# Attention and two MLPs on one core: the low-part subtraction moved from GpSimd to VectorE, some softmax quotients to ScalarE

## The chip, the cores and the metric

The kernel runs on one core of a Trainium2 chip. The metric is the device time of one execution in microseconds. The core has five engines with an instruction queue each: TensorE (PE in the profile; its weight loads are PEld), VectorE (DVE), ScalarE (ACT), GpSimd (POOL) and SyncE (SP), which here only starts DMA transfers.

## The reference

```python
# q, k, v: (4, 8, 576, 64); all inputs and outputs fp32
scores = scale * q @ k.T                      # per batch and head
masks: heads 0-3: 0 <= i - j < 32; heads 4-7: 0 <= i - j < 128 and (i - j) % 4 == 0
attn = softmax(where(mask, scores, -1e9))
x = (attn @ v) reshaped to (2304, 512)
x = relu(x @ w_in) ** 2 @ w_out               # first MLP, 512 -> 2048 -> 512
h = x @ w_in2; out = (h * cos(h)) @ w_out2    # second MLP, same sizes
```

## The kernel before

**Matmuls in parts.** Every fp32 factor of the two MLPs is held as a high part, which TensorE's fast fp32 format holds exactly, and a low part, the rest. A product is three matmuls: high by high, high by low, low by high.

**Weights.** A weight chunk (128 x 512) arrives as 64-bit words over SyncE (`load_w`, line L105; three buffers `raw`). `split_w` makes fp32 words of them with three VectorE instructions (L116, L119, L122) in a tile `wt` with two buffers, ScalarE casts that to the high part (L125), and GpSimd subtracts the high part from `wt` to give the low part (L127). There are 32 chunks for each MLP (16 values of `fc`, `i` = 0 and 1), and the second MLP's chunks go into the tiles of the first's, so each waits until the last block of the first MLP has used the tile.

**Blocks.** The 2304 tokens go through each MLP in five blocks of 512 or 384 (`SIZES`). For each `fc` a block has `product1` (12 matmuls, L306), `middle` and `product2` (12 matmuls, L363). `middle` of the first MLP is a relu (L318), a square (ScalarE L321 or VectorE L337), the high part (ScalarE L346) and the low part (VectorE L348). In the second MLP it has L324, a rounding step on GpSimd (L325), L328, L330, L333, L334, L337, L346 and L348.

**Attention.** It is cut into 48 units. A unit has scores (L198), for the later units a mask (L215), a maximum (L219), three exponentials with row sums on ScalarE (L225), the sum's reciprocal (L230, L231), the quotient (L232), a transpose (L237), a copy (L240), the product with the values (L249) and the two parts of the result (L276 on ScalarE, L278 on VectorE). The first 12 units (`first`) run ahead of the MLP and have their quotient on GpSimd. The other 36 are spread over the blocks of the first MLP, and have theirs on VectorE.

**Order.** Each step is written down at a time `t` counted in steps of `fc` (block k of the first MLP begins at 16 k), and the list is sorted by these times. The stretches before t = 0 and from t = 96 on are issued as written. Between them, where the first MLP and the second one's first block lie, a planner orders each engine's instructions by its own costs, with the written order as priority. `SPLIT` holds the times of the four steps of `split_w` after its start; early chunks (six) have times of their own. Splits are half a step of `fc` apart in the first MLP.

Of the kernel before, what the change touches and what calls it, by code (L numbers as in the profile page):

```python
# [11 lines left out]
AF = mybir.ActivationFunctionType  # L12
ALU = mybir.AluOpType
# [3 lines left out]
P = 128  # L17
# [6 lines left out]
KT = 96  # L24
TPU = 3
# [11 lines left out]
NF = DFF // P  # L37
# [19 lines left out]
def attention_moe_moe(ctx: ExitStack, tc: tile.TileContext, units, masks, ident16_in, ident_in, w1, w2, out):  # L57
    nc = tc.nc
# [16 lines left out]
    f32 = lambda ap: ap.bitcast(F32)  # L75
# [4 lines left out]
    def at(t, f, *a):  # L80
        events.append((t, len(events), f, a))
# [26 lines left out]
    def split_w(m, fc, i):  # L108


        words = raws.pop((m, fc, i))
        low, high = words[:, :, 0], words[:, :, 1]
        parts = wpool.tile([P, 2, DM], F32R, tag=f"w{fc}_{i}", name=f"w{fc}_{i}")
        hi, lo = weights[m, fc, i] = parts[:, 0, :], parts[:, 1, :]
        t = wtmp.tile([P, DM], U32, tag="t", name="wt")
        nc.vector.tensor_scalar(  # L116
            out=t, in0=high, scalar1=3, scalar2=0x3FFFFFF8,
            op0=ALU.logical_shift_left, op1=ALU.bitwise_and)
        nc.vector.scalar_tensor_tensor(  # L119
            out=t, in0=high, scalar=0xC0000000, in1=t, op0=ALU.bitwise_and, op1=ALU.bitwise_or)  # L120
        yield
        nc.vector.scalar_tensor_tensor(  # L122
            out=t, in0=low, scalar=29, in1=t, op0=ALU.logical_shift_right, op1=ALU.bitwise_or)
        yield
        nc.scalar.copy(out=hi, in_=f32(t))  # L125
        yield
        nc.gpsimd.tensor_tensor(out=lo, in0=f32(t), in1=f32(hi), op=ALU.subtract)  # L127
        yield


# [2 lines left out]
    def block(m, k):  # L133
        if (m, k) not in xs:
            s = SLOT[k]
            xs[m, k] = tuple(
                ring.tile([P, NC, SIZES[k]], F32R, tag=f"x{n}{s}", name=f"x{n}{s}") for n in "hl"
            )
        return xs[m, k]
# [32 lines left out]
    def bank():  # L172
        return ps_h.tile([P, 512], F32, tag="h", name="h")

    def y_bank(e):
        return ps_y.tile([P, 512], F32, tag=f"y{e}", name=f"y{e}")

    def warm_up(n):

        spare = bank()  # L180
        for _ in range(n):
            nc.tensor.matmul(spare, idle[:, :P], idle, start=True, stop=True)

    def unit(u):


        first = u < N_EARLY
        b, hp, g = u // UNITS, u % UNITS // NG, u % NG
        dilated = hp >= NPAIR // 2
        x, v = loaded.pop(u)  # L190
        s = bank()[:, :TPU * KT]
        m0 = MASK_OF[dilated][g] * KT
        m = mask[:, m0:m0 + TPU * KT]
        if u == 0:
            warm_up(7)
        for i in range(TPU):
            for j in range(0, P, D):
                nc.tensor.matmul(  # L198
                    s[j:j + D, i * KT:(i + 1) * KT],
                    x[j:j + D, i:UQ:TPU],  # L200
                    x[j:j + D, UQ + i * QT:UQ + i * QT + KT],
                    start=not first or i == 0, stop=not first,
                )
        if first:
            nc.tensor.matmul(s, ident16, m, start=False, stop=True)
        if u == 1:
            warm_up(6)
        yield
        p = ppool.tile([P, TPU, KT], F32, tag="p", name="p")
        scale = 1.0 / D ** 0.5  # L210
        tiles = lambda t: t.rearrange("p (i k) -> p i k", k=KT)
        if first:
            s = tiles(s)
        else:
            nc.vector.scalar_tensor_tensor(  # L215
                out=p, in0=tiles(s), scalar=scale, in1=tiles(m), op0=ALU.mult, op1=ALU.add)
            s, scale = p, 1.0
        nm = stat.tile([P, TPU], F32, tag="nm", name="nm")
        nc.vector.tensor_reduce(out=nm, in_=s, axis=AX.X, op=ALU.max, negate=True)  # L219
        if first:  # L220
            nc.vector.tensor_scalar(out=nm, in0=nm, scalar1=scale, scalar2=None, op0=ALU.mult)
        yield
        sm = stat.tile([P, TPU], F32, tag="sm", name="sm")
        for i in range(TPU):
            nc.scalar.activation(  # L225
                out=p[:, i, :], in_=s[:, i, :], func=AF.Exp, scale=scale,
                bias=nm[:, i:i + 1], accum_out=sm[:, i:i + 1])
        yield
        rs = stat.tile([P, TPU], F32, tag="rs", name="rs")
        nc.vector.tensor_scalar(out=rs, in0=sm, scalar1=EPS, scalar2=None, op0=ALU.add)  # L230
        nc.vector.reciprocal(out=rs, in_=rs)  # L231
        (nc.gpsimd if first else nc.vector).tensor_tensor(  # L232
            out=p, in0=p, in1=rs.unsqueeze(2).to_broadcast([P, TPU, KT]), op=ALU.mult)
        yield
        pt = bank()[:KT, :UP]
        for i in range(TPU):
            nc.tensor.transpose(pt[:, i * 2 * QT:(i + 1) * 2 * QT], p[:, i, :], ident)  # L237
        yield
        pts = ptpool.tile([KT, UP], F32, tag="pts", name="pts")
        nc.scalar.copy(out=pts, in_=pt)  # L240
        yield
        pv = y_bank(u % 4) if first else bank()
        if not first:
            v = loaded.pop(u)
        for i in range(TPU):
            for j in range(2):
                at_q = (i * 2 + j) * QT
                at_v = (i * 2 + j) * D
                nc.tensor.matmul(  # L249
                    pv[j * D:(j + 1) * D, i * QT:(i + 1) * QT],  # L250
                    v[:, at_v:at_v + D],
                    pts[:, at_q:at_q + QT],
                    start=True, stop=True,
                )
        yield

        p0 = g * TPU * QT
        done = 0
        pieces = []
        while done < TPU * QT:  # L260
            if dilated:
                r, i0 = divmod(p0 + done, S // DIL)
                n, step = min(TPU * QT - done, S // DIL - i0), DIL
                t0 = b * S + DIL * i0 + r
            else:
                n, step = TPU * QT - done, 1
                t0 = b * S + p0 + done
            k = max(i for i in range(NB) if STARTS[i] <= t0)
            t0 -= STARTS[k]
            n = min(n, -(-(SIZES[k] - t0) // step))  # L270
            xh, xl = (t[:, hp, t0:t0 + (n - 1) * step + 1:step] for t in block(0, k))
            piece = pv[:, done:done + n]
            pieces.append((xh, xl, piece))
            done += n
        for xh, _, piece in pieces:
            nc.scalar.copy(out=xh, in_=piece)  # L276
        for xh, xl, piece in pieces:
            nc.vector.tensor_tensor(out=xl, in0=piece, in1=f32(xh), op=ALU.subtract)  # L278
        yield
# [10 lines left out]
    def in_steps(times, key, steps, *a):  # L290
        for i, t in enumerate(times):
            at(t, *((resume, key) if i else (start, key, steps, *a)))
# [119 lines left out]
    def needed(u):  # L412
        b, hp, g = u // UNITS, u % UNITS // NG, u % NG
        t = b * S + (g * TPU * QT if hp < NPAIR // 2 else 0)
        return max(i for i in range(NB) if STARTS[i] <= t)

    later = sorted(range(N_EARLY, UNITS * B), key=lambda u: (needed(u), u))
    place = []
    for k, (n, t, span) in enumerate(((10, 0.051, 14.1), (12, -0.15, 13), (10, 0.04, 14), (4, 0.051, 12))):
        place += [k * NF + t + span * i / n for i in range(n)]  # L420

    def later_by(t, d):

        while d:
            k = int(t // NF) if d > 0 else -int(-t // NF) - 1
            pace = PACE[k % NB]
            edge = (k + 1) * NF - t if d > 0 else k * NF - t
            move = d / pace
            if abs(move) <= abs(edge):
                return t + move  # L430
            t += edge
            d -= edge * pace
        return t
    for u in range(UNITS * B):
        if u < N_EARLY:
            t = 1.3 * u if u < 2 else 3.877 + 1.656 * (u - 2)
            times = [before(t + d) for d in (0, 1, 2.07, 2.87, 4.24, 4.95, 5.32, 6.2)]
        else:
            t = place[later.index(u)]
# [6 lines left out]

    EARLY_LOADS = (2.5, 3.5, 6.62, 8.91, 10.16, 11.56)
    EARLY_SPLITS = (5.5, 7, 17.91, 21.32, 23.16, 24.98)
    SPLIT = (0, 0.05, 0.2, 0.3)
    split_at = []  # L450
    for h in range(2 * NF):
        w = (0, h // 2, h % 2)
# [3 lines left out]
        else:  # L456
            t = h / 2 - 1.573
            times = [t + d for d in SPLIT]
            at(split_at[h - 3] + 0.01 if h >= RAW_EARLY + 3 else before(-1. + 0.01 * h), load_w, *w)
# [9 lines left out]
    for h, (t, w) in enumerate(split_at):  # L469
        in_steps([t + d for d in SPLIT], ("w", *w), split_w, *w)  # L470
        at(t - 1.5, load_w, *w)
    for m in range(2):
        for k in range(NB):
            t = (m * NB + k) * NF
# [98 lines left out]
```

## Time and profile before

| | us |
|---|---|
| median of 3 runs | 942.76 (942.71 to 943.51) |
| profiled execution: its time | 943.5 |
| its span, first to last instruction | 941.7 |
| busy PE / DVE / ACT / POOL | 904.4 / 546.8 / 445.5 / 148.9 |
| mean granted TensorE clock | 0.982 of full |

The span is what the trace covers; 1.8 us of the execution's time lie around it. Busy time is the time in which an engine ran at least one instruction. Work that TensorE does at a granted clock below 1 takes longer and counts as busy too.

### The profile page before, as it was taken

What the parts mean: (1) busy time and instruction counts of PE and PEld (TensorE: products, weight loads), DVE (VectorE), ACT (ScalarE), POOL (GpSimd) and SP (SyncE); (2) the same over time, 40 slices, a digit from 0 to 9 for tenths busy, and PEclk for the clock granted to TensorE, in tenths of its full rate; (3) what the DMA queues carried; (4) which work ended last, traced back from release to release, by engine and by line L of the source; (5) the groups of instructions that cost most, each with busy time, mean ns of one, the idle gap of its engine ahead of it and who ended that gap; (6) DMA issues with size and microseconds to landing.
All of it is one profiled execution on the core that took longest, in us unless ns stands there. A gap on an engine that the chain in (4) does not pass through costs nothing.

```text
span 941.7 us, 13625 instructions
## 1 busy us (share of the span) xinstructions
PE 904.4 (96%) x5161; PEld 772.7 (82%) x5161; DVE 546.8 (58%) x1019; ACT 445.5 (47%) x1062; POOL 148.9 (16%) x160
## 2 busy tenths in 40 slices
PE   7898799999999999999987899999999999999998
PEld 5576577999887777888987788889998888888998
DVE  5899962445343435332599887455555565455554
ACT  4765554445343433322444465445554544545553
POOL 2444430000000000000254422111111111111110
PEclk8999899999999999999999899999999999999999
DMA  9756521222121113000456431002002002000100
GB/s 249 219 163 203 181 82 32 94 54 57 29 74 34 44 29 128 1 0 1 145 173 200 130 123 34 1 1 90 1 6 75 1 0 79 1 1 1 45 1 34
DMA packets 27680, 66.28 MB, mean 70 GB/s; under 512 B 3168, under 2 KB 15328, under 8 KB 27616
## 3 DMA queue, kind: packets, MB, share of 16 engines
q1 hardware_dynamic: 27616, 65.42, 22.7%
q8 instruction: 41, 0.67, 0.3%
q14 instruction: 23, 0.19, 0.1%
HBM read 55.97 MB, written 9.44 MB: 69 GB/s over the span
## 4 chain that ended last, share of the span: by engine, by line
PE 68%; DVE 15%; issue 11%; DMA 3%; POOL 1%; ACT 1%; SPq 0%; POOLq 0%; ACTq 0%; DVEq 0%
PE y L363 32%; PE h L306 31%; DVE wt L119 4%; DVE wt L116 3%; DMA early<-units 3%; DVE wt L122 3%; PE h L198 2%; PE h L249 2%; DVE gl L348 1%; PE h L237 1%; POOL kf L325 1%; DVE r L330 1%; POOL w L127 1%; DVE p L232 1%; DVE r L328 1%
## 5 line engine op out<-in xcount | busy, mean ns | idle before, releaser
L363 PE MATMUL y<-gh,w 128*128 128x512 f32 (+1 forms) x1280 | 400.6, 374 | 4.1 <-ACT gh L346 2.1
L306 PE MATMUL h<-xh,w 128*128 128x512 f32 (+1 forms) x1280 | 402.4, 375 | 1.2 <-DVE xl L278 0.9
L363 PEld LDWEIGHTS y<-gh,w 128*128 128x128 f32 x1280 | 240.7, 190 | 36.4 <-ACT gh L346 2.6
L306 PEld LDWEIGHTS h<-xh,w 128*128 128x128 f32 x1280 | 241.1, 190 | 33.8 <-PE y L363 1.3
L363 PE MATMUL y<-gl,w 128*128 128x512 f32 (+1 forms) x640 | 238.5, 373 | 11.3 <-DVE gl L348 11.2
L306 PE MATMUL h<-xl,w 128*128 128x512 f32 (+1 forms) x640 | 238.0, 372 | 0.0
L348 DVE TENSOR_TENSOR gl<-r,gh 128x512 fp32r<-128x512 f32 (+1 forms) x160 | 107.8, 674 | 118.9 <-ACT gh L346 118.5
L337 DVE TENSOR_TENSOR r<-h,r 128x512 f32<-128x512 f32 (+1 forms) x128 | 81.9, 640 | 158.7 <-ACT r L334 96.0
L127 POOL TENSOR_TENSOR w<-wt,w 128x512 fp32r<-128x512 f32 x64 | 93.4, 1463 | 428.2 <-ACT w L125 428.2
L363 PEld LDWEIGHTS y<-gl,w 128*128 128x128 f32 x640 | 121.8, 190 | 28.7 <-DVE gl L348 13.9
L306 PEld LDWEIGHTS h<-xl,w 128*128 128x128 f32 x640 | 121.9, 191 | 14.8
L346 ACT CAST gh<-r 128x512 fp32r<-128x512 f32 (+1 forms) x160 | 92.0, 575 | 88.8 <-PE y L363 72.8
L333 ACT ACTIVATE r<-r 128x512 f32<-128x512 f32 (+1 forms) x80 | 47.2, 590 | 148.1 <-DVE r L330 148.1
L325 POOL TENSOR_SCALAR kf<-kf 128x512 f32<-128x512 f32 (+1 forms) x80 | 47.5, 594 | 327.9 <-ACT kf L324 320.7
L318 ACT ACTIVATE r<-h 128x512 f32<-128x512 f32 (+1 forms) x80 | 44.3, 553 | 96.9 <-PE h L306 96.6
L125 ACT CAST w<-wt 128x512 fp32r<-128x512 f32 x64 | 39.6, 620 | 76.3 <-DVE wt L122 76.1
L122 DVE SCALAR_TENSOR_TENSOR wt<-wraw,wt 128x512 uint32<-128x512 uint32 x58 | 60.9, 1050 | 1.0
L324 ACT ACTIVATE kf<-h,magic 128x512 f32<-128x512 f32 (+1 forms) x80 | 51.1, 639 | 20.9 <-PE h L306 20.0
L334 ACT ACTIVATE r<-r,halfpi 128x512 f32<-128x512 f32 (+1 forms) x80 | 54.5, 681 | 2.5
L225 ACT ACTIVATE p<-p,nm 128x96 f32<-128x96 f32 x108 | 39.5, 366 | 33.2 <-DVE nm L219 33.2
L330 DVE SCALAR_TENSOR_TENSOR r<-kf,r 128x512 f32<-128x512 f32 (+1 forms) x80 | 53.2, 665 | 2.6
L328 DVE SCALAR_TENSOR_TENSOR r<-kf,h 128x512 f32<-128x512 f32 (+1 forms) x80 | 50.1, 626 | 7.8 <-POOL kf L325 7.8
(49 smaller groups left out, 528.2 us busy)
## 6 DMA issues: line engine op xcount, KB each, us to landing
wraw<-w SPq DMA_DIRECT2D x58, 512.0 KB, 3.6
uq<-units SPq DMA_DIRECT2D x36, 208.0 KB, 2.6
uv<-units SPq DMA_DIRECT2D x36, 144.0 KB, 2.2
early<-w SPq DMA_DIRECT2D x6, 512.0 KB, 9.6
y<-o SPq DMA_DIRECT2D x6, 512.0 KB, 2.8
xraw<-y SPq DMA_DIRECT2D x6, 512.0 KB, 4.9
out<-o SPq DMA_DIRECT2D x6, 512.0 KB, 2.8
early<-units SPq DMA_DIRECT2D x12, 208.0 KB, 9.2
```

Source lines behind the costliest of these rows:

```text
L122: nc.vector.scalar_tensor_tensor(out=t, in0=low, scalar=29, in1=t, op0=ALU.logical_shift_right, op1=ALU.bitwise_or)
L127: nc.gpsimd.tensor_tensor(out=lo, in0=f32(t), in1=f32(hi), op=ALU.subtract)
L306: nc.tensor.matmul(h, w[:, c * P:(c + 1) * P], x[:, c, :], start=c == 0 and i == 0, stop=c == NC - 1 and i == 2)
L324: nc.scalar.activation(out=kf, in_=h, func=AF.Identity, bias=magic, scale=INV2PI)
L325: nc.gpsimd.tensor_scalar(out=kf, in0=kf, scalar1=-MAGIC, scalar2=1.0, op0=ALU.add, op1=ALU.mult)
L328: nc.vector.scalar_tensor_tensor(out=r, in0=kf, scalar=-C1, in1=h, op0=ALU.mult, op1=ALU.add)
L330: nc.vector.scalar_tensor_tensor(out=r, in0=kf, scalar=-C2, in1=r, op0=ALU.mult, op1=ALU.add)
L334: nc.scalar.activation(out=r, in_=r, func=AF.Sin, bias=halfpi, scale=-1.0)
L337: nc.vector.tensor_tensor(out=r, in0=h, in1=r, op=ALU.mult)
L346: nc.scalar.copy(out=gh, in_=r)
L348: nc.vector.tensor_tensor(out=gl, in0=r, in1=f32(gh), op=ALU.subtract)
L363: nc.tensor.matmul(y[e], w[:, e * P:(e + 1) * P], g, start=fc == 0 and n == 0, stop=fc == NF - 1 and n == 2,)
```

## The change

The low parts of all weight chunks are subtracted on VectorE, so that it runs all of `split_w` but the cast. The quotient of the first 12 units moves from GpSimd to VectorE. The quotient of the 11 later units that begin beside the first block (`place` below 16) moves from VectorE to ScalarE, as three activations with a scale for each row. The last step of a split is written at 0.62 in place of 0.3. GpSimd has then no work in the first MLP; in the second it keeps L325.

```diff
@@ split_w
         nc.scalar.copy(out=hi, in_=f32(t))
         yield
-        nc.gpsimd.tensor_tensor(out=lo, in0=f32(t), in1=f32(hi), op=ALU.subtract)
+        nc.vector.tensor_tensor(out=lo, in0=f32(t), in1=f32(hi), op=ALU.subtract)
         yield
@@ unit
         nc.vector.reciprocal(out=rs, in_=rs)
-        (nc.gpsimd if first else nc.vector).tensor_tensor(
-            out=p, in0=p, in1=rs.unsqueeze(2).to_broadcast([P, TPU, KT]), op=ALU.mult)
+        if u in with_weights:
+            for i in range(TPU):
+                nc.scalar.activation(
+                    out=p[:, i, :], in_=p[:, i, :], func=AF.Copy, scale=rs[:, i:i + 1])
+        else:
+            nc.vector.tensor_tensor(
+                out=p, in0=p, in1=rs.unsqueeze(2).to_broadcast([P, TPU, KT]), op=ALU.mult)
@@ after place
+    with_weights = {u for u, t in zip(later, place) if t < NF}
@@
-    SPLIT = (0, 0.05, 0.2, 0.3)
+    SPLIT = (0, 0.05, 0.2, 0.62)
```

## Rows read from the trace of the kernel before

**Rows 1.** Stages: length, then each engine's busy time (instructions), clock, DMA share, GB/s.
```profile
10.00:40.00 30.00, 25.52 (x300) 18.80 (x301) 24.19 (x78) 21.52 (x101) 12.02 (x16) 0.89 1.01 280
40.00:130.00 90.00, 76.28 (x463) 58.56 (x461) 87.06 (x152) 49.38 (x139) 41.33 (x29) 0.92 0.52 164
130.00:464.00 334.00, 333.76 (x2097) 279.28 (x2098) 136.61 (x333) 128.07 (x393) 3.83 (x3) 1.00 0.16 48
464.00:538.00 74.00, 62.67 (x322) 59.59 (x321) 70.90 (x86) 33.57 (x66) 34.89 (x24) 0.93 0.55 173
```

**Rows 2.** Chain that ended last, by line: 40 to 130 us, then 464 to 538 us.
```profile
by line: DVE wt L119 20.4%; issue 20.3%; DVE wt L122 17.1%; DVE wt L116 15.7%; DVE p L232 5.6%; DVE gl L348 3.8%; POOL w L127 3.7%; DVE xl L278 3.5%; DVE p L215 3.4%; ACT w L125 2.1%; DVE nm L219 2.0%; DVE rs L230 1.0%; DVE rs L231 0.7%; AC
...
by line: issue 35.5%; DVE wt L119 24.8%; DVE wt L116 15.3%; DVE gl L348 9.5%; DVE wt L122 9.4%; POOL w L127 1.8%; ACT w L125 1.7%; DVE xl L396 1.3%; ACT xh L395 0.7%; PE y L363 0.6%
```

**Rows 3.** Timeline, 68 to 77 us: start, length, engine, instruction.
```profile
68.06 0.68 DVE L122 SCALAR_TENSOR_TENSOR wt<-wraw,wt 128x512 uint32<-128x512 uint32 x1
68.66 0.42 DVE L116 TENSOR_SCALAR wt<-wraw 128x512 uint32<-128x512 uint32 x1
...
69.47 1.49 POOL L127 TENSOR_TENSOR w<-wt,w 128x512 fp32r<-128x512 f32 x1 [3.27 <-ACT w L125]
...
69.84 1.67 DVE L122 SCALAR_TENSOR_TENSOR wt<-wraw,wt 128x512 uint32<-128x512 uint32 x1
...
73.61 0.19 ACT L225 ACTIVATION_READ_ACCUMULATOR p<-p,nm 128x1 f32 x1
...
76.21 0.17 DVE L231 RECIPROCAL rs<-rs 128x3 f32<-128x3 f32 x1
```

**Rows 4.** VectorE's groups, 40 to 130 us: busy us, mean ns, idle before.
```profile
L122 DVE SCALAR_TENSOR_TENSOR wt<-wraw,wt 128x512 uint32<-128x512 uint32 x26 | 26.1, 1004 | 0.2
L119 DVE SCALAR_TENSOR_TENSOR wt<-wraw,wt 128x512 uint32<-128x512 uint32 x26 | 21.2, 820 | 0.3
L116 DVE TENSOR_SCALAR wt<-wraw 128x512 uint32<-128x512 uint32 x26 | 15.4, 599 | 2.4 <-POOL w L127 2.4
L232 DVE TENSOR_TENSOR p<-p,rs 128x288 f32<-128x288 f32 x8 | 10.1, 1261 | 0.0
```

**Rows 5.** VectorE's groups, 200 to 400 us, where GpSimd ran nothing.
```profile
L348 DVE TENSOR_TENSOR gl<-r,gh 128x512 fp32r<-128x512 f32 x23 | 15.9, 690 | 23.3 <-ACT gh L346 23.0
...
L232 DVE TENSOR_TENSOR p<-p,rs 128x288 f32<-128x288 f32 x19 | 8.7, 458 | 0.7
...
L348 DVE TENSOR_TENSOR gl<-r,gh 128x384 fp32r<-128x384 f32 x10 | 5.6, 557 | 11.1 <-ACT gh L346 11.1
...
L122 DVE SCALAR_TENSOR_TENSOR wt<-wraw,wt 128x512 uint32<-128x512 uint32 x2 | 1.4, 688 | 0.0
L116 DVE TENSOR_SCALAR wt<-wraw 128x512 uint32<-128x512 uint32 x2 | 0.8, 418 | 0.0
```

**Rows 6.** VectorE's groups, 464 to 538 us.
```profile
L122 DVE SCALAR_TENSOR_TENSOR wt<-wraw,wt 128x512 uint32<-128x512 uint32 x23 | 27.5, 1195 | 0.7
L119 DVE SCALAR_TENSOR_TENSOR wt<-wraw,wt 128x512 uint32<-128x512 uint32 x23 | 20.1, 872 | 0.7
L116 DVE TENSOR_SCALAR wt<-wraw 128x512 uint32<-128x512 uint32 x23 | 11.8, 511 | 1.3 <-POOL w L127 1.3
L348 DVE TENSOR_TENSOR gl<-r,gh 128x384 fp32r<-128x384 f32 x13 | 11.5, 882 | 1.8 <-ACT gh L346 1.8
```

**Rows 7.** GpSimd's groups: 40 to 130 us, then 464 to 538 us.
```profile
L127 POOL TENSOR_TENSOR w<-wt,w 128x512 fp32r<-128x512 f32 x29 | 43.1, 1490 | 49.9 <-ACT w L125 49.9
...
L127 POOL TENSOR_TENSOR w<-wt,w 128x512 fp32r<-128x512 f32 x24 | 34.9, 1457 | 43.0 <-ACT w L125 43.0
```

**Rows 8.** ScalarE's groups, 40 to 130 us.
```profile
L125 ACT CAST w<-wt 128x512 fp32r<-128x512 f32 x28 | 17.4, 620 | 33.9 <-DVE wt L122 33.8
L225 ACT ACTIVATE p<-p,nm 128x96 f32<-128x96 f32 x24 | 8.8, 366 | 2.4 <-DVE nm L219 2.4
```

**Rows 9.** DMA issues of the whole span: count, size, median us to landing.
```profile
wraw<-w SPq DMA_DIRECT2D x58, 512.0 KB, 3.6
```

## Prediction

> **What bounds the kernel now.** I read first the stages of the span. From 130 to 464 us TensorE is busy 333.76 of 334 us, so nothing done elsewhere in that stretch can shorten it. Two stretches are different: from 40 to 130 us TensorE is idle 13.7 us and VectorE is busy 87.06 of 90, and from 464 to 538 us TensorE is idle 11.3 us and VectorE is busy 70.90 of 74 [rows 1]. These are the stretches in which the weights of the two MLPs are split. TensorE's granted clock is 0.92 and 0.93 of full there, so it spent part of them on the lower of its two levels, behind its own waits [rows 1].
>
> Then the chain that ended last in both. Nearly all of it is VectorE: the three passes of the split and, as "issue", time in which VectorE ran without a release that the profile shows [rows 2]. TensorE stands for less than one per cent of the second. So in these two stretches, 164 us long, the time is VectorE's sum.
>
> Then the length of the same VectorE instruction. L122 takes 0.68 us at 68.06, and 1.67 us at 69.84, where a subtraction of GpSimd that began at 69.47 and ended at 70.96 overlaps it [rows 3]; what is left of 1.67 after 70.96 is 0.55, about the whole work. The same is seen in the means: where GpSimd runs nothing, L122 takes 688 ns and L116 418 [rows 5]; in the first stretch 1004 and 599, in the second 1195 and 511 [rows 4, 6]. L119 is the same operation on as many elements as L122, and I take 690 for it undisturbed; it takes 820 and 872 [rows 4, 6]. The quotient on VectorE takes 458 ns alone and 1261 here [rows 4, 5]. VectorE so pays for GpSimd's subtractions by standing still behind them.
>
> **What is taken off VectorE, first stretch.** L122: 26 x (1004 - 688) ns = 8.2 us. L119: 26 x (820 - 690) = 3.4. L116: 26 x (599 - 418) = 4.7. Eight quotients leave VectorE altogether: 10.1, less 0.08 each by which neighbours on VectorE overlap (L122 of 0.68 us began 0.60 before the next [rows 3]), so 9.4. L116's idle time behind GpSimd: 2.4 [rows 4]. Sum 28.1 us.
>
> **What is put on it.** The subtraction on VectorE has not run before. The nearest row is L348, the same subtraction with the same kinds of operands on 512 columns: 690 ns alone [rows 5], hence 0.61 from start to start. GpSimd did 29 of them in the stretch [rows 7]: 17.7 us, or 20.0 if nothing overlapped. Net: 10.4 us less (8.1 to 10.4).
>
> **The start.** From 10 to 40 us the loads fill the DMA engines (share 1.01) while VectorE is busy 24.19 of 30 [rows 1]. GpSimd's 16 instructions of that stage, twelve quotients and four subtractions, come onto VectorE, the former at 0.38 each (458 ns less the overlap), the latter at 0.61: 7.0 us more. It costs nothing if waits for loads cover all of it and 7.0 if they cover none; VectorE's 5.8 us of idle time there are mostly such waits, so I take the rest, 1.2. Each early quotient loses the way to GpSimd and back, which I count at nothing since loads end last there.
>
> **Second stretch.** L122: 23 x (1195 - 688) = 11.7 us. L119: 23 x (872 - 690) = 4.2. L116: 23 x (511 - 418) = 2.1. L348 on 384 columns: 13 x (882 - 557) = 4.2. Wait on GpSimd: 1.3 [rows 5, 6]. Sum 23.5. Added: 24 subtractions [rows 7] at 0.61, so 14.6 (16.6 without overlap). Net 8.9 less (6.9 to 8.9). The remaining splits of the second MLP lie where TensorE is full, and count for nothing; L325 stays on GpSimd there and goes on disturbing VectorE.
>
> **The wait that is added.** On VectorE the subtraction waits for ScalarE's cast, and all of VectorE's queue waits behind it: the next split, L348, on which TensorE's `product2` waits, and through the freed `raw` buffers SyncE's next load. On GpSimd nothing stood behind that wait. Straight behind its cast it would cost the cast's 620 ns [rows 8] and two handovers, some 0.75 us, 53 times, 40 us; with the next split's passes in between (0.60 + 0.60 + 0.34 = 1.5 us of work) it costs nothing. In the written order the next split lies between, its passes at 0.50 and 0.55 after this split's start and the subtraction at 0.62. The planner orders by its own costs, so I take neither end but 3.5 us in all, near the lower one since ScalarE is busy only 49.38 of 90 and 33.57 of 74 us [rows 1].
>
> **The quotients on ScalarE.** Three activations on 96 columns; the nearest row is the exponential of the same shape, 366 ns [rows 8], so at most 1.1 us for each unit, 8.8 us for eight in a stretch where ScalarE has 40.6 idle [rows 1]. Nothing on the path, as long as ScalarE's queue is not held. The three other units run where TensorE is full: nothing. The Trainium skill ("ScalarE: Activation LUTs", Rules for kernel authors) speaks against this edit: multiplications belong on VectorE, not on ScalarE. By the figure of the same page (What ACT_TABLE_LOAD costs) for an activation with one pointer operand, 280 ns + 0.833 ns for each column, the three would be estimated at 1.08 us against 0.46 on VectorE, a loss of 5 us over eight units if ScalarE set the time; by the rows it does not.
>
> **SyncE.** No transfer is added. A split comes every 2.4 to 2.7 us in place of about 3.1, and with three buffers a load has two splits' time, some 5 us, to land. It takes 3.6 [rows 9]. Nothing, with little to spare.
>
> **TensorE's own bound.** At full clock its work in the stretches would take 76.28 x 0.92 = 70 us of 90 and 62.67 x 0.93 = 58 of 74. VectorE's new sums, about 80.8 and 65.1, lie above both, so the cut counts in full.
>
> **Sum.** 10.4 + 8.9 - 1.2 - 3.5 = 14.6 us off 943.5, the time of the profiled execution (span 941.7 and 1.8 around it): 928.9. The median of the runs is 0.7 lower than that execution, so 928.2.
>
> **Rivals.**
> 1. *Subtractions stand behind their casts (slower).* Mean wait w over 53 subtractions. At w = 0.34 us the 18.1 us before this allowance are used up; at 0.75 the time is 942.8 + 40 - 18.1 = 965. For it: VectorE's order is not the written one but the planner's, and ScalarE waits for L122 for 33.8 us in the stretch [rows 8], so casts begin as soon as L122 ends and a subtraction next in line would find its cast just begun. Against it: there is always another split to run. 9 in 100.
> 2. *ScalarE is held at the quotient.* In the written order the three activations follow the exponentials at once and wait for the reciprocal on VectorE. At 73.80 the sums were there and only at 76.38 the reciprocal: 2.6 us [rows 3]. Casts and L346 would wait behind. With eight such waits passed on to VectorE at half their length 10 us go, and the time is 939. This is also how the Trainium skill's rule on multiplications would be felt. Against it: ScalarE's idle time, 40 us. 13 in 100, for 934 to 941.
> 3. *TensorE gains more.* With fewer waits its clock stays full, and VectorE's dependent passes leave gaps that subtractions can fill. TensorE's idle time and clock together are worth at most (90 - 70) + (74 - 58) = 36 us; half of that, 18 to 24 in all, gives 919 to 925. 12 in 100.
> 4. *No change:* the gain and a new wait cancel, or the lengthening of VectorE's passes has another cause than GpSimd, and the added 32 us stand against 9.4 and the waits. Against the latter: rows 3 and 5. 4 in 100 for no change, 2 for slower.
>
> The forecast, 925 to 934, has 60 in 100. Within 0.2% (1.9 us, about what a measurement can tell from nothing) lies 4 in 100; slower 11; faster 85. From 919 to 938 leaves out the slower and unchanged cases and a little of rivals 2 and 3.
>
> **What would show it.** GpSimd has no instruction before the second MLP. L122 and L119 fall to about 0.69 us and L116 to 0.42 in the first stretch; the subtraction takes 0.69. VectorE stays full up to about 121 us in place of 130, and TensorE waits for L348 for less than now in the second stretch, which ends some 16 us earlier than 538. Idle time of VectorE put down to L125 is small, 3 to 4 us. If that is tens of microseconds, or ScalarE idles behind L231 and VectorE behind ScalarE, the prediction is wrong by rivals 1 and 2. If L122 stays at 1 us in the first stretch, the reading of rows 3 was wrong.

## The result and the profile after

The changed kernel takes 904.88 us (median of 4 runs, 903.73 to 906.05) against 943.13 (942.71 to 944.14) for the kernel before beside it: ratio 0.9593, 95% interval 0.9576 to 0.961. It is 38 us faster. The forecast was 928.2 with a range of 919 to 938, so the direction was right and the gain more than twice what was forecast.

The page of the changed kernel, its busy times and the chain that ended last (the profiled execution took 906.05 us, its span is 904.3):

```profile
PE 888.5 (98%) x5161; PEld 762.1 (84%) x5161; DVE 528.7 (58%) x1084; ACT 454.1 (50%) x1095; POOL 47.9 (5%) x84
...
PE 87%; DMA 5%; DVE 5%; ACT 1%; issue 1%; SPq 0%; ACTq 0%; DVEq 0%
```

TensorE was busy 904.4 us and idle 37.3 of the span; now it is busy 888.5 and idle 15.8. So 21.5 us come from idle time of TensorE and 15.9 from the same 5161 matmuls taking less time; the mean clock rose from 0.982 to 0.998. That is the whole gain.

Stages of the changed kernel, with the columns of [rows 1] (the second stretch now lies earlier, so it is shown from 410 to 520 us):

```profile
10.00:40.00 30.00, 25.10 (x323) 18.55 (x325) 28.38 (x96) 21.76 (x101) 0.00 (x0) 1.00 0.92 278
40.00:130.00 90.00, 86.98 (x560) 68.16 (x557) 82.72 (x191) 66.50 (x196) 0.00 (x0) 1.00 0.59 174
...
410.00:520.00 110.00, 108.40 (x559) 100.27 (x559) 84.08 (x147) 55.44 (x104) 2.69 (x4) 0.98 0.48 154
```

From 40 to 130 us TensorE was busy 76.28 us at a clock of 0.92 [rows 1]; it is now busy 86.98 at 1.00. The chain of that stretch, by line, was VectorE [rows 2] and is now TensorE:

```profile
by line: PE h L311 42.0%; PE y L368 37.5%; PE h L198 6.2%; PE h L254 5.0%; PE h L242 4.5%; ACT w L125 1.3%; ACT r L323 1.2%; DVE wt L122 0.7%; ACT r L326 0.6%; ACT gh L351 0.6%; ACT xh L281 0.5%; ACT p L225 0.4%; issue 0.1%
```

VectorE's groups from 40 to 130 us, which answer to [rows 4]; L127 is the subtraction, new on VectorE:

```profile
L127 DVE TENSOR_TENSOR w<-wt,w 128x512 fp32r<-128x512 f32 x28 | 19.1, 685 | 1.2 <-ACT w L125 0.8
L122 DVE SCALAR_TENSOR_TENSOR wt<-wraw,wt 128x512 uint32<-128x512 uint32 x26 | 17.8, 684 | 0.0
L119 DVE SCALAR_TENSOR_TENSOR wt<-wraw,wt 128x512 uint32<-128x512 uint32 x26 | 17.7, 682 | 0.1
L116 DVE TENSOR_SCALAR wt<-wraw 128x512 uint32<-128x512 uint32 x26 | 10.9, 420 | 1.8 <-DMA wraw<-w 1.8
```

L122 fell from 1004 to 684 ns, L119 from 820 to 682, L116 from 599 to 420, and the subtraction takes 685: each is the prediction's value within 10 ns. The timeline around the same place as [rows 3] shows split passes of two chunks and a low part of the hidden layer (L353) one behind the other, none longer than 0.69:

```profile
67.95 0.68 DVE L119 SCALAR_TENSOR_TENSOR wt<-wraw,wt 128x512 uint32<-128x512 uint32 x1
68.55 0.68 DVE L353 TENSOR_TENSOR gl<-r,gh 128x512 fp32r<-128x512 f32 x1
69.16 0.68 DVE L122 SCALAR_TENSOR_TENSOR wt<-wraw,wt 128x512 uint32<-128x512 uint32 x1
...
70.53 0.69 DVE L127 TENSOR_TENSOR w<-wt,w 128x512 fp32r<-128x512 f32 x1
71.14 0.69 DVE L122 SCALAR_TENSOR_TENSOR wt<-wraw,wt 128x512 uint32<-128x512 uint32 x1
```

What TensorE waits for, over the whole span: first two groups of the kernel before, then the three that answer to them after.

```profile
L363 PE MATMUL y<-gl,w 128*128 128x512 f32 (+1 forms) x640 | 238.5, 373 | 11.3 <-DVE gl L348 11.2
...
L237 PE MATMUL h<-ident,p 128*96 128x128 f32 x144 | 25.6, 288 | 11.6 <-DVE p L232 9.6 <-POOL p L232 1.5 <-ACT xh L276 0.5
```

```profile
L368 PE MATMUL y<-gh,w 128*128 128x512 f32 (+1 forms) x1280 | 397.4, 372 | 4.0 <-ACT gh L351 4.0
L368 PE MATMUL y<-gl,w 128*128 128x512 f32 (+1 forms) x640 | 236.0, 369 | 0.2 <-DVE gl L353 0.2
...
L242 PE MATMUL h<-ident,p 128*96 128x128 f32 x144 | 24.9, 280 | 1.4 <-DVE p L237 0.9 <-ACT p L225 0.4
```

The waits for VectorE's low part (11.2 us) and for its quotient (9.6) have fallen to 0.2 and 0.9 us.

**Where along the span.** Each block ends with copies of its sums by VectorE (L376 before, L381 after). The start of the first of them, and the time from block to block, place the gain:

| us | before | after |
|---|---|---|
| end of block 1 of the first MLP | 169.3 | 149.6 |
| blocks 2, 3, 4 | 91.1, 104.3, 93.1 | 91.1, 104.3, 93.3 |
| block 5 (second MLP's weights split beside it) | 86.1 | 71.9 |
| first block of the second MLP | 92.0 | 87.7 |
| the four blocks after it | 68.6, 86.8, 85.3, 60.7 | 69.0, 86.8, 85.3, 60.7 |

So 19.7 us come from the first stretch and 18.5 from the second. The prediction had 9.2 and 8.9, less 3.5 for both.

**What stands between two points.** Take the first stretch from the first to the eleventh low part of the hidden layer (L348 before, L353 after). Stage and VectorE's L122 in it, before:

```profile
47.50:130.00 82.50, 70.99 (x417) 54.92 (x416) 79.59 (x135) 45.08 (x125) 37.46 (x26) 0.92 0.55 173
...
L122 DVE SCALAR_TENSOR_TENSOR wt<-wraw,wt 128x512 uint32<-128x512 uint32 x26 | 26.1, 1004 | 0.2
```

and after:

```profile
45.90:107.60 61.70, 61.67 (x386) 48.76 (x387) 58.96 (x133) 47.19 (x137) 0.00 (x0) 1.00 0.68 201
...
L122 DVE SCALAR_TENSOR_TENSOR wt<-wraw,wt 128x512 uint32<-128x512 uint32 x21 | 14.4, 684 | 0.0
```

The stretch fell from 82.5 to 61.7 us, and in it TensorE is busy 61.67 of 61.7. But it is not the same stretch of work on VectorE: it holds 21 splits and not 26. Counted in the order of VectorE's instructions, 32 splits stand in front of the eleventh low part before, 27 after. The planner gives VectorE its order by its own costs; with a subtraction more in each split it puts fewer of them in front of the same hidden-layer step, and the others run behind it, up to about 127 us. Beside block 5 it is the same: 55 splits stand in front of the thirteenth low part before, 50.5 after. The prediction counted the same splits in the same place. TensorE's order is new too: 417 matmuls lie between the two points before and 386 after. So the 20.8 us between them overstate the gain: from the first low part to the end of block 1 it takes 121.8 us before and 103.7 after, 18.1 less.

### The profile page after: what moved, and what is told of

Its sections match the earlier page's. It is cut to its first block, busy times and chain, and to the rows that moved or that the text cites. A ratio compares the mean times of both kernels' runs of the same rounds, so it can differ in the third digit from the quotient of the medians.

```text
span 904.3 us, 13572 instructions
## 1 busy us (share of the span) xinstructions
PE 888.5 (98%) x5161; PEld 762.1 (84%) x5161; DVE 528.7 (58%) x1084; ACT 454.1 (50%) x1095; POOL 47.9 (5%) x84
## 4 chain that ended last, share of the span: by engine, by line
PE 87%; DMA 5%; DVE 5%; ACT 1%; issue 1%; SPq 0%; ACTq 0%; DVEq 0%
PE y L368 41%; PE h L311 40%; PE h L198 3%; DMA early<-units 3%; PE h L254 2%; DMA wraw<-w 2%; PE h L242 2%; DVE wt L119 1%; DVE wt L122 1%; DVE w L127 1%; DVE wt L116 1%; DVE gl L353 1%; DMA xraw<-y 0%; DMA y<-o 0%; DVE xl L283 0%
## 5 line engine op out<-in xcount | busy, mean ns | idle before, releaser
L311 PE MATMUL h<-xh,w 128*128 128x512 f32 (+1 forms) x1280 | 398.1, 372 | 0.4 <-ACT xh L281 0.4
L368 PEld LDWEIGHTS y<-gh,w 128*128 128x128 f32 x1280 | 238.1, 188 | 36.2 <-ACT gh L351 4.8
L311 PEld LDWEIGHTS h<-xh,w 128*128 128x128 f32 x1280 | 237.6, 188 | 31.9 <-ACT xh L281 0.6
L368 PE MATMUL y<-gl,w 128*128 128x512 f32 (+1 forms) x640 | 236.0, 369 | 0.2 <-DVE gl L353 0.2
L353 DVE TENSOR_TENSOR gl<-r,gh 128x512 fp32r<-128x512 f32 (+1 forms) x160 | 102.4, 640 | 114.4 <-ACT gh L351 114.0
L125 ACT CAST w<-wt 128x512 fp32r<-128x512 f32 x64 | 39.5, 619 | 33.4 <-DVE wt L122 32.8
L335 DVE SCALAR_TENSOR_TENSOR r<-kf,r 128x512 f32<-128x512 f32 (+1 forms) x80 | 50.9, 638 | 2.5
L127 DVE TENSOR_TENSOR w<-wt,w 128x512 fp32r<-128x512 f32 x64 | 43.6, 685 | 5.4 <-ACT w L125 5.0
L122 DVE SCALAR_TENSOR_TENSOR wt<-wraw,wt 128x512 uint32<-128x512 uint32 x58 | 40.6, 699 | 0.3
```

The lines of the kernel that those rows point to most:

```text
L122: nc.vector.scalar_tensor_tensor(out=t, in0=low, scalar=29, in1=t, op0=ALU.logical_shift_right, op1=ALU.bitwise_or)
L127: nc.vector.tensor_tensor(out=lo, in0=f32(t), in1=f32(hi), op=ALU.subtract)
L311: nc.tensor.matmul(h, w[:, c * P:(c + 1) * P], x[:, c, :], start=c == 0 and i == 0, stop=c == NC - 1 and i == 2)
L335: nc.vector.scalar_tensor_tensor(out=r, in0=kf, scalar=-C2, in1=r, op0=ALU.mult, op1=ALU.add)
L353: nc.vector.tensor_tensor(out=gl, in0=r, in1=f32(gh), op=ALU.subtract)
L368: nc.tensor.matmul(y[e], w[:, e * P:(e + 1) * P], g, start=fc == 0 and n == 0, stop=fc == NF - 1 and n == 2,)
```

## The experiments

Every ratio is to the kernel before run beside it on the same chip. "Low part" is that of the hidden layer (`gl`); "order" means how many splits stand in front of which low part in VectorE's queue.

**Which part of the change, and which stretch.** `sub_first` is the changed kernel with the second MLP's subtractions on GpSimd, as before; `sub_second` is the kernel before with only those on VectorE; `sub_both` has all subtractions on VectorE (written at 0.62) and the quotients as before; `quot_only` has the quotients as changed and the subtractions on GpSimd (at 0.3). The diff is cut to the lines of the subtraction.

```diff
@@ sub_first: changed kernel (SPLIT 0.3 for the second MLP); sub_second: kernel before (0.62 for it)
-        nc.vector.tensor_tensor(out=lo, in0=f32(t), in1=f32(hi), op=ALU.subtract)
+        (nc.gpsimd if m else nc.vector).tensor_tensor(...)     # sub_first
+        (nc.vector if m else nc.gpsimd).tensor_tensor(...)     # sub_second
```

> The subtraction is on VectorE for the first MLP's weights alone; the second MLP's stay on GpSimd with the old step 0.3; quotients as in the changed kernel. If the two stretches of weight splitting gain each for itself, this keeps the first one's gain: by the two traces TensorE's work is some 20 us ahead after it, so about 923 us. If the gain of one stretch depends on the other (loads or splits run further ahead), it is under 915 or over 932.

> The kernel before with the subtraction on VectorE for the second MLP's weights alone (step 0.62 there). If the stretches gain each for itself, about 926 us (17 us less), and with the run above the two gains add up to 38 us. If the recorded sum was right and only the first stretch was mis-sized, about 934.

> The subtraction on VectorE with its step at 0.62; all quotients stay where they were (first 12 units GpSimd, the others VectorE). By the rows eight quotients at 0.38 us come back to VectorE in the first stretch, 3 us, and GpSimd disturbs it in the first 40 us. If the subtraction is the whole matter: 905 to 909. If ScalarE's quotients carry part of the first stretch's gain, 912 to 920.

> The quotients as in the changed kernel, the subtraction on GpSimd with its step at 0.3. By the recorded sum VectorE loses 9.4 us in the first stretch: 933 to 936. If the time that the quotients stood behind GpSimd only passes to the next instruction, VectorE wins 3 us (eight at 0.38): 938 to 942. If ScalarE is held by the wait for the reciprocal: above 943.

| | us | ratio (95%) |
|---|---|---|
| sub_first | 925.73 | 0.9826 (0.9791 to 0.986) |
| sub_second | 922.71 | 0.979 (0.9761 to 0.9819) |
| sub_both | 905.97 | 0.9605 (0.9586 to 0.9624) |
| quot_only | 947.28 | 1.0044 (1.0026 to 1.0063) |

17.3 and 20.3 us for the stretches add up to 37.6, the whole gain: as far as intervals of some 3 us to each side can tell, the two are independent. `sub_second` lies well under the 934 that was expected if only the first stretch had been mis-sized; both were. The subtraction alone brings 36.4; the quotients with it about 1 us more, which the intervals don't tell from nothing, and by themselves they cost 4 to 5. In the profile of `quot_only`, from 40 to 130 us, this is what TensorE's transpose (L242) waits for, and ScalarE's quotient (L234):

```profile
L242 PE MATMUL h<-ident,p 128*96 128x128 f32 x27 | 6.7, 328 | 8.4 <-ACT p L234 8.4
```

```profile
L234 ACT ACTIVATE p<-p,rs 128x96 f32<-128x96 f32 x21 | 6.3, 364 | 4.3 <-DVE rs L231 4.2
```

With GpSimd still holding VectorE the reciprocal (L231) comes late, ScalarE stands for 4.2 us at the quotient, and TensorE 8.4 us behind that: the mechanism of rival 2. But it only takes the place of the 9.6 us for which the transposes waited for VectorE's quotient before. From the first low part to the end of block 1 it takes 175.2 - 53.5 = 121.7 us, before 169.3 - 47.5 = 121.8. The 6 us that this execution loses lie ahead of the first low part, where TensorE has half its clock from 20 to 30 us (columns as in [rows 1]):

```profile
20.00:30.00 10.00, 9.90 (x86) 7.03 (x87) 5.87 (x25) 5.28 (x25) 0.00 (x0) 0.50 1.05 308
```

Whether the early quotients on VectorE bring this about, or the scatter of that stage (below, the start), was not settled.

**GpSimd's reads put back.** `lock_back` is the changed kernel with a useless subtraction on GpSimd, 448 columns into a scrap tile, behind each split. VectorE's instructions and their order are exactly those of the changed kernel (the scrap tile's own line is left out of the diff).

```diff
         nc.vector.tensor_tensor(out=lo, in0=f32(t), in1=f32(hi), op=ALU.subtract)
+        nc.gpsimd.tensor_tensor(
+            out=scrap, in0=f32(hi)[:, :448], in1=f32(hi)[:, :448], op=ALU.subtract)
```

> The changed kernel, and behind each subtraction on VectorE GpSimd runs a useless one: it reads 448 columns of the high part twice and writes a scrap tile nobody reads. VectorE's instructions stand in exactly the order of the changed kernel. Theory one, VectorE standing still behind GpSimd's reads is the whole cost: L122, L119 and L116 grow to the means of before, VectorE has its new subtractions besides, and the time is 935 to 950. Theory two, the planner's new order is what helped (the high and low parts of the hidden layer no longer wait behind splits that run ahead): VectorE's passes grow the same, TensorE loses little, and the time is 905 to 918. If GpSimd's reads do nothing to VectorE: 905.

934.28 us, ratio 0.9905 (0.9881 to 0.993): 29 of the 38 us are lost again. That is just under theory one's 935 to 950 and far from theory two's 905 to 918. VectorE's groups and GpSimd's, 40 to 130 us (lines are one or two further down; L128 is the subtraction, L123 was L122):

```profile
L128 DVE TENSOR_TENSOR w<-wt,w 128x512 fp32r<-128x512 f32 x25 | 23.0, 925 | 0.0
L123 DVE SCALAR_TENSOR_TENSOR wt<-wraw,wt 128x512 uint32<-128x512 uint32 x23 | 19.0, 824 | 0.0
L120 DVE SCALAR_TENSOR_TENSOR wt<-wraw,wt 128x512 uint32<-128x512 uint32 x23 | 18.7, 814 | 0.0
```

```profile
L129 POOL TENSOR_TENSOR scrap<-w 128x448 bf16<-128x448 f32 x25 | 32.3, 1292 | 60.9 <-ACT w L126 59.6 <-ACT xh L283 1.3
```

A GpSimd instruction that nobody waits for lengthens VectorE's passes to 814 to 925 ns on average. VectorE does stand still behind GpSimd's reads. In the profiled execution it takes 111.6 us from the first low part to the end of block 1 (103.7 in the changed kernel) and block 5 takes 86.1 (71.9); 5 us more lie ahead of the first low part, in the stage whose scatter is told below.

**GpSimd without reads.** `no_read` is the kernel before with the subtraction replaced by a GpSimd memset of the low part; it leaves out the low parts of the weights, and with them the wait for ScalarE's cast. VectorE's order is nearly that of the kernel before (32 splits in front of the eleventh low part in both).

```diff
-        nc.gpsimd.tensor_tensor(out=lo, in0=f32(t), in1=f32(hi), op=ALU.subtract)
+        nc.gpsimd.memset(f32(lo), 0.0)
```

> The kernel before, with GpSimd's subtraction replaced by a memset of the low part to zero: it leaves out the low parts of the weights, GpSimd writes as much as before and reads nothing, and the splits run ahead of L348 as before on VectorE (same counts within half a split). Theory one: VectorE's passes fall to 0.69 and 0.42 us and the time to 905 or less, since VectorE has not even the subtractions. Theory two: L348 still stands behind splits, and the time is 912 to 930. If GpSimd's writes hold VectorE too, above 930.

911.83 us, ratio 0.9658 (0.9617 to 0.9699). VectorE's L122, 40 to 130 us and then 430 to 520 us, where the memsets run beside it:

```profile
L122 DVE SCALAR_TENSOR_TENSOR wt<-wraw,wt 128x512 uint32<-128x512 uint32 x26 | 17.8, 685 | 0.1
...
L122 DVE SCALAR_TENSOR_TENSOR wt<-wraw,wt 128x512 uint32<-128x512 uint32 x25 | 17.3, 691 | 0.8
```

Without the reads, with nothing put on VectorE and in nearly the order of before, it is 31 us faster; that lies between theory one (905 or less) and theory two (912 to 930), at the edge of the second. From the first to the eleventh low part it takes 64.9 us (82.5 before), TensorE busy for 63.22. This kernel keeps its eight quotients on VectorE, at some 0.38 us each, so the prediction's first-stretch terms without its subtractions give 82.5 - 28.1 + 3.0 = 57.4 for VectorE (it was busy for 58.22): already below what TensorE needs. VectorE's L116 waits 5.0 us of this stretch for weight loads.

**The order alone.** `before_held` is the kernel before, GpSimd's subtractions and all, with each split's first pass queued on VectorE behind the low part that it follows in the changed kernel (the table of these places is left out of the diff).

```diff
+        if behind:     # low parts in front of this split in the changed kernel
+            tc.add_manual_dep(first_pass.ins, lows[behind[-1]].ins.name, ..., reason="order of after")
```

> The kernel before, subtractions on GpSimd, with one constraint: the first pass of each split is queued on VectorE behind the low part of the hidden layer that it stands behind in the kernel after (27 splits in front of the eleventh low part in place of 32). It tests the order alone, with GpSimd's reads still in the way. Theory one (VectorE's sum is shortened by the lock's end, and the order only decides how much of it stands in front of a hidden-layer step): between the two low parts VectorE had 79.6 us of work; five splits fewer at about 2.9 us each take 14 off, so the first stretch gets some 8 to 14 us shorter, the second likewise where TensorE's waits allow, 918 to 932 in all, L122 still near 1 us. Theory two (the order is worth nothing, the whole gain is the end of the lock): 938 to 945. Theory three (the order is the whole gain): 903 to 912.

928.83 us, ratio 0.9842 (0.9816 to 0.9868). The order alone is worth 14.6 us even with GpSimd's reads in the way, as theory one had it. Block 1 ends at 155.3 in place of 169.3; block 5 takes 86.2 and the next 91.9, as before. So by itself the order counts in the first stretch and not in the second. Block 5 of `lock_back`, with the changed kernel's order, takes 86.1 as well: with GpSimd's reads in the way it takes that in either order. From the first to the eleventh low part:

```profile
45.70:114.90 69.20, 66.36 (x393) 52.12 (x393) 64.61 (x121) 41.27 (x116) 28.98 (x20) 0.95 0.57 184
```

```profile
L135 DVE SCALAR_TENSOR_TENSOR wt<-wraw,wt 128x512 uint32<-128x512 uint32 x20 | 15.0, 751 | 0.0
...
L361 DVE TENSOR_TENSOR gl<-r,gh 128x512 fp32r<-128x512 f32 x10 | 12.0, 1198 | 4.4 <-ACT gh L359 4.4
```

GpSimd's reads now fall on other instructions: L135 (L122 before) is at 751 ns, the low part at 1198 where it had 677 in the same stretch of the kernel before.

**The order of before with the subtraction on VectorE.** This is nearly the kernel that the prediction's sum was made for. `order_as_before` is the changed kernel with the splits written earlier and closer together, shortly ahead of the times at which the low parts that they precede in the kernel before are written (`ahead` looks these up; its tables are left out of the diff).

```diff
-            t = h / 2 - 1.573
+            t = ahead(FIRST, h + 1) - 0.6
@@ second MLP's splits
+        if 2 < h < 27:
+            t = t1 - NF + ahead(LAST, 33 + h) - 0.8
```

> The kernel after, the subtraction on VectorE, with the splits written earlier and closer together, so that as many of them stand in front of each low part of the hidden layer on VectorE as in the kernel before: in the first block 12, 19, 24.5, 28 and 31.5 in front of the fourth, sixth, eighth, tenth and eleventh (before 12.5, 18, 24, 29.5 and 32; after 11.5, 16, 20.5, 24.5 and 27), in the second stretch 52 in front of the thirteenth (before 55, after 50.5). It is the kernel that the prediction's sum was made for: five splits more in front of the eleventh low part, 2.15 us of VectorE's work each. Theory one (the sum was right for that order, and the miss is the order): the first stretch gets 7 to 11 us longer than after, the second 2 to 4, 914 to 922 in all; by the prediction's sum as it stands 928. Theory two (VectorE's sum is too long in the prediction whatever the order, and the order is worth nothing once GpSimd is silent): 903 to 910.

914.5 us, ratio 0.9696 (0.968 to 0.9712): 9.6 us above the changed kernel, inside theory one's range and outside theory two's. Block 1 ends at 156.8 (after 149.6), block 5 takes 73.3 (71.9), the next 88.8 (87.7). Stages, first between the first and the eleventh low part, then beside block 5 between the first and the thirteenth:

```profile
47.50:119.70 72.20, 69.83 (x426) 53.35 (x427) 68.42 (x151) 50.67 (x145) 0.00 (x0) 0.98 0.64 200
...
442.60:496.70 54.10, 54.10 (x310) 53.59 (x309) 47.19 (x88) 30.13 (x59) 0.00 (x0) 1.00 0.63 204
```

The latter stretch of the kernel before, and of the changed kernel:

```profile
455.80:525.10 69.30, 60.37 (x312) 57.94 (x312) 62.71 (x80) 32.36 (x63) 30.75 (x21) 0.93 0.63 197
```

```profile
435.50:487.50 52.00, 52.00 (x298) 51.49 (x297) 45.73 (x83) 30.41 (x59) 0.00 (x0) 1.00 0.67 213
```

What VectorE and TensorE wait for in the first stretch:

```profile
L116 DVE TENSOR_SCALAR wt<-wraw 128x512 uint32<-128x512 uint32 x25 | 10.5, 422 | 2.0 <-DMA wraw<-w 1.9
...
L368 PE MATMUL y<-gl,w 128*128 128x512 f32 x39 | 16.3, 419 | 2.4 <-DVE gl L353 2.4
```

In the first stretch VectorE is nearly full (68.42 of 72.2), and 72.2 is the prediction's 82.5 - 10.4 = 72.1. But TensorE is busy for 69.83 us of it, and the chain that ended last goes through TensorE's two products for 35.6% and through weight loads for 16.2%: VectorE's work has the size of the sum, but VectorE alone does not set the length. In the second TensorE is full (54.10 of 54.1) and VectorE has 6.9 us to spare, with 52 of the 55 splits of before in front of the thirteenth low part (closer than that the written times did not bring it). Three more splits at 2.15 us would still fit into these 6.9 us.

**Room on VectorE.** `sub_twice` does the subtraction twice on VectorE.

```diff
         nc.vector.tensor_tensor(out=lo, in0=f32(t), in1=f32(hi), op=ALU.subtract)
+        nc.vector.tensor_tensor(out=lo, in0=f32(t), in1=f32(hi), op=ALU.subtract)
```

> The kernel after with the subtraction of each split done twice on VectorE (same operands, same result). It adds 53 instructions of about 0.61 us in the two stretches, 32 us, to VectorE alone. Theory one (TensorE is the bound of both stretches after the change, and splits that find no room move behind the hidden-layer steps to where VectorE is idle): between the first and the eleventh low part 20 splits add 12 us and VectorE had 2.7 us free, two splits fewer in front give 5.6 back, so about 4 us for a stretch, 907 to 920 in all. Theory two (as the prediction has it, VectorE's sum sets the length of both stretches, so that all that is put on it counts in full): 905 + 32 = 937, at least 930.

916.33 us, ratio 0.9706 (0.9682 to 0.973): 11.4 us more and not 32. It lies inside theory one's range. From the first to the eleventh low part it takes 69.0 us, now with 25 splits in front of the eleventh:

```profile
49.40:118.40 69.00, 68.13 (x421) 52.17 (x421) 65.29 (x144) 47.01 (x139) 0.00 (x0) 0.98 0.55 171
```

Two splits fewer than in the changed kernel stand in front again, and two thirds of the work added to VectorE don't show in the time.

**Three other places for the splits.** `early_step` has the subtraction written at 0.3 as before; `splits_ahead` has all but the first splits written 1.5 steps earlier, `later_start` 0.6 later, in both MLPs (the diff shows the first).

```diff
-    SPLIT = (0, 0.05, 0.2, 0.62)
+    SPLIT = (0, 0.05, 0.2, 0.3)        # early_step
-            t = h / 2 - 1.573
+            t = h / 2 - 3.073              # splits_ahead; later_start: h / 2 - 0.973
```

> The changed kernel with the last step of a split written at 0.3 again. VectorE's order by the planner is nearly the same (948 of 1084 instructions stand in the same place). If the subtraction had to be kept from standing right behind its cast by the written time, VectorE waits for L125 and the time is 912 or more; if the planner does that by itself, 905.

> The changed kernel with all later splits written 1.5 steps earlier. The planner then puts 16 to 28 splits in front of the low parts of the hidden layer number 5 to 11 in place of 13.5 to 27 (before: 15.5 to 32), and about 1.5 more in the second stretch. Theory two, in the reduced form that is left (with the subtraction on VectorE the time also rests on how many splits stand in front of L353): two splits of 2.2 us each in each stretch, 908 to 914. If VectorE's order does not matter once GpSimd is silent: 905.

> The kernel after with all splits behind the first six written later by 0.6 of a step, in both MLPs; one split fewer stands in front of some low parts. A candidate for a faster version. Theory one (TensorE is full from 50 to 510 us already, and only the ends, where it waits for ScalarE, have something to give): 901 to 907. Theory two (the place of the splits in VectorE's queue still counts by some 2 us each): 895 to 901.

907.81 (ratio 0.9625, 0.9606 to 0.9645), 910.93 (0.9659, 0.9636 to 0.9682) and 910.26 (0.9655, 0.9615 to 0.9694). None is better than the changed kernel. `early_step` lies between its two expected times, `splits_ahead` in theory two's range, `later_start` above both of its ranges. The written time of the subtraction is worth some 3 us at most: VectorE's idle time behind the cast (L125) is 5.5 us over the span with 0.3 and 5.0 with 0.62. For `later_start` the profiled execution (span 905.6) shows no difference that would explain its other runs, up to 913.3; this stays open.

## Why the prediction was wrong in size, point by point

**VectorE stands still behind GpSimd's subtractions: right.** Every duration came out (684, 682, 420, 685 ns), and `lock_back` and `no_read` show the cause from both sides. The Trainium skill ("SBUF — State Buffer", Who interferes with whom) calls it an exclusive lock of a port pair that the two engines share; [rows 3] agree, where L122 has 0.55 of its 0.68 us left when GpSimd's subtraction ends, and so does `lock_back`, where reads of 1.29 us on GpSimd stretch passes of 0.68 us to 0.81 to 0.93 on average.

**The net of the first stretch, 10.4 us: of the right size for the order it was worked out for.** With nearly the order of before, the stretch up to the eleventh low part takes 72.2 us where the sum gives 72.1. That they agree to 0.1 us is luck in part, since TensorE and the loads share in that length; from the first low part, at 47.5 in both, to the end of block 1 it gains 121.8 - 109.3 = 12.5 us, 2.1 more than the term.

**"VectorE's new sums, about 80.8 and 65.1, lie above both, so the cut counts in full": this step failed**, in two ways. It took VectorE's instructions in a stretch as given. They are not: the order is made anew, and 27 splits stand in front of the eleventh low part where 32 did. Five splits at four passes of 0.60 + 0.60 + 0.60 + 0.34 = 2.15 us each, some 10.7 us, went behind it, and VectorE was busy 58.96 us up to there in place of the 68.42 of `order_as_before`. So VectorE's sum fell under TensorE's 61.67, and TensorE is full from 50 us on. (The stretch itself fell from 72.2 to 61.7, but TensorE also did 386 matmuls in it in place of 426; by the end of block 1 the difference is 109.3 - 103.7 = 5.6 us.) And it took the length of the second stretch, 74 us, as VectorE's sum, where VectorE was busy for 70.90 [rows 1]: its idle time, 3.1 us there and 69.3 - 62.7 = 6.6 between the first and the thirteenth low part (2.1 behind TensorE, 1.8 behind ScalarE, 1.3 behind GpSimd), was waits for others and not its own work. With VectorE's own work alone TensorE was the bound there at once: in `order_as_before`, TensorE is busy for 54.10 of 54.1 us and VectorE for 47.19, or some 53.6 with the three splits that are missing there.

**The sum.** Of the 38 us, 28.0 come with nearly the order of before (942.48 to 914.5) and 9.6 from the order. The 28.0 is, within 0.5, the forecast's 14.6 with 2.1 more in the first stretch, 16.0 - 8.9 = 7.1 more in the second (blocks 5 and the next, 178.1 to 162.1), and the 1.2 and 3.5 that were set aside for the start and the waits, which did not come: 28.5. Taken the other way round, the order brings 14.6 first (`before_held`) and the rest about 24 (928.83 to 904.88), so the shares depend on which comes first. Nor need all of the 9.6 be the order: `early_step`, with nearly the order of the changed kernel, is 2.9 us slower than it. How the order's share divides for the second stretch is not settled, since `before_held` gains nothing there and `order_as_before` has only part of the order of before.

**The wait for the cast, 3.5 us: of the right size, and without effect.** VectorE is idle behind L125 for 0.8 us of the first stretch's subtractions and 5.0 over the span. Rival 1 (the subtractions behind their casts) did not come.

**The quotients on ScalarE at nothing: right** together with the subtraction (TensorE waits 1.4 us ahead of all transposes). `quot_only` shows rival 2's wait where VectorE is late, in place of another of the same length. The Trainium skill ("ScalarE: Activation LUTs", Rules for kernel authors) advises against the edit, as it gives multiplications to VectorE. Alone the edit came out 4 to 5 us slower, but the profile doesn't show these at the quotients, and with the subtraction on VectorE no cost can be seen.

**The start, 1.2 us: not to be told.** VectorE is busy 28.38 of the 30 us from 10 to 40, 4.2 more than before, and the first low part comes at 45.9 in place of 47.5; but in the profiles of this study it starts between 45.7 and 53.5 us, with granted clocks of 0.72 to 1.00 in that stage, and kernels alike in it differ.

**SyncE at nothing: right.** A load takes 4.3 us in place of 3.6 [rows 9], and L116 waits 1.8 us for it in the first stretch. That little is to spare was right too: the wait is 5.0 us in `no_read`. Its 2.4 us for a split are not what its own sums give (79.6 / 29 and 65.1 / 24, both 2.7); measured are 61.7 / 21 = 2.9.

**Rival 3 was the case, and more of it.** It put TensorE's idle time and clock at up to 36 us and took half. All of it came: 21.5 us of idle time and 15.9 of busy time. TensorE's idle time and its mean clock go together in the first stretch: 11.5 us at 0.92 before, 2.8 at 0.95 in `before_held`, 2.4 at 0.98 in `order_as_before`, 0.03 at 1.00 after. That subtractions fill gaps between dependent passes, which the rival also named, no run isolates.

## What to carry to other kernels

Where a planner makes the order, a stretch's sum of an engine is not a constant: before adding up what an edit puts on an engine and takes off it, find which of its instructions the next waiting engine really needs before it goes on, and which can slide behind. When the bound's relief is larger than the distance to the next engine's own need, the time ends at that need; work that distance out first, with the clock that the next engine has when it no longer waits, and set the forecast there unless something holds the sum up. And a read on GpSimd can cost VectorE as much as it saves: look at the same VectorE instruction with and without GpSimd beside it.

## What the runs showed of the hardware that was not expected

GpSimd's memset of 128 x 512 (0.54 us) does not lengthen VectorE's two-input passes: L122 takes 691 ns from 430 to 520 us of `no_read`, beside 32 memsets, and 688 alone [rows 5]. The L122 at 450.07, which a memset from 450.02 to 450.55 overlaps, takes 0.69 us. Only the subtraction, which reads, lengthened them.

The stand-still seems to go the other way too. In `sub_twice`, where VectorE runs its passes without a gap at the beginning of the second MLP, GpSimd's rounding step up to 538 us:

```profile
L331 POOL TENSOR_SCALAR kf<-kf 128x512 f32<-128x512 f32 x5 | 9.3, 1859 | 526.4 <-ACT kf L330 526.4
```

It takes 1859 ns there on average (from 0.62 to 4.64 us; spans on GpSimd are rough) and 621 ns in the changed kernel from 560 to 900 us. VectorE's passes beside it keep their times but for two, an L122 of 1.08 us and an L116 of 0.85 in place of 0.42. Which of the two engines stands still seems to depend on which is back to back, and no run here isolates it.
